# Attention, mixture of experts and dense layer in one kernel: a smaller second run and two decoded units moved ahead of a branch

## The chip, the cores and the metric

One core of a Trainium2 chip runs the whole program in one launch. The metric is the device time of that launch in microseconds (us). The kernel before took 637.18 us, the median of three executions (636.78 to 637.54).

The engines are named as the profile names them: PE is TensorE (matrix products), DVE is VectorE, ACT is ScalarE, POOL is GpSimd, SP is SyncE, which here issues most of the DMAs.

## The reference

```python
attn = softmax(rot(q) @ rot(k).T / 8) @ v          # 2 x 8 heads, 576 rows, 64 columns
x    = attn as 1152 rows x 512                     # all heads of a row side by side
nl   = x @ w_gate + log1p(exp(x @ w_noise)) * noise    # 8 experts
top2 = two largest of nl in each row, weights = softmax over the two
for each expert e, for its rows:  out += weight * (relu(x @ w1[e]) @ w2[e])   # 512 -> 1024 -> 512
h = out @ w_in                                     # 512 -> 2048, w_in and w_out in 64-bit floats
y = (max(h, 0) + log1p(exp(-|h|))) @ w_out         # 2048 -> 512
```

Everything is computed in 32-bit precision: a product of two 32-bit matrices is made of three products of a high and a low part (high by high, high by low, low by high).

## The kernel before

The kernel has three stages in time. Up to about 168 us it computes the attention, in an order that is written out by hand: the string `ORDER` names each piece of work, and the engines take their pieces in that order (each engine works strictly in its own order). `plan` gives for every piece its engine and what has to stand ahead of it.

From 168 to about 423 us it works through nine runs of expert rows. Run 0 takes one expert's rows of the first 512 tokens, and is part of `ORDER` (`G0` to `G7`), so that it starts before the routing of all tokens is known. Runs 1 to 8 take the eight experts in order of their number of rows. Run 1 takes what is left of run 0's expert, with the same weights. `CAPS` gives the rows each run has room for, 192 for run 0 and 256 for run 1 in the kernel before; `RTILES` the 128-row tiles they make (two for both). An expert with more rows than that is completed by `overflow()`, under a branch (line 1447) that tests `mxi`, the largest excess. All five engines load `mxi` (line 1446) and take the branch each for itself. When it isn't taken, each engine adds to its own semaphores what the skipped instructions would have added, after its own earlier instructions have ended.

A run is 14 to 17 slots. The first eight are `gemm1` (line 1264 on): for each 128 of the 1024 hidden columns, 12 products (4 pieces of 512 by 3 parts) over all rows of the run. Then comes `gemm2`: for each tile of rows 24 products 512 columns wide, three parts with a slot after each. A tile of at most 64 rows has another form (lines 1290 to 1297): high and low part of its rows lie side by side in one stationary operand, and two products of a kind take the place of three, 16 in all. `xg_T` transposes the gathered rows of the next run in between.

In the slots the other engines prepare what comes: `split_hi` and `split_lo` (lines 189 and 193) split a 512 KB chunk of weights into high and low part, on ACT and DVE. The 64-bit matrices are decoded in 32 units: `dec_load` (a DMA on SP's queue, lines 215 and 218), `dec_a` (two ACT instructions, lines 227 and 228), `dec_b` (two DVE instructions, lines 235 and 236, and one on POOL, line 239), `dec_c` (a DMA to `wtab`, line 244). `dec_at` says in which slot each step stands; the first two units were loaded just ahead of run 1 and decoded in it.

From 423 us to the end the dense layer runs on `wtab`.

The memory of the attention's pools is given to later pools. `pa` holds the two output tiles of run 0 (`y0`, `y1`) and is closed before `mo`, which holds among others the row buffers `xg` of the gathers, the outputs `y`, and the eight buffers `hb` of `gemm1`'s results.

Of the kernel before, what the change touches and what calls it, by code (L numbers as in the profile page):

```python
# [11 lines left out]
F32 = mybir.dt.float32  # L12
# [3 lines left out]
I32 = mybir.dt.int32  # L16
U32 = mybir.dt.uint32
AF = mybir.ActivationFunctionType
OP = mybir.AluOpType
# [4 lines left out]
B, H, S, D = 2, 8, 576, 64  # L24
N, DM, E, F1 = B * S, H * D, 8, 1024
# [3 lines left out]

CAPS = (192, 256, 256, 288, 288, 320, 320, 320, 384)
NR = len(CAPS)
RTILES = [-(-c // 128) for c in CAPS]
ROW0 = [sum(RTILES[:r]) for r in range(NR)]
# [52 lines left out]
T14,5 Th14,4 X12 Th14,5 Tl14,4 X13 E70 Tl14,5 E71 T15,0 Xd12 T15,1 rs15 Th15,0 Xd13 l12 A14,1 Th15,1 Tl15,0 l13 ld3  # L88
sl1 Tl15,1 T15,4 Ao14,1 A14,0 Th15,4 XT0 Tl15,4 Ao14,0 z1 T15,2 XTh0 sl2 Th15,2 T15,3 XTl0 A15,0 Th15,3 Tl15,2 Tl15,3
XT1 Ao15,0 XTh1 A15,1 sp3 XTl1 ri14 ld5 X14 sl3 Ao15,1 sp4 X15 Xd14 ri15 l14 ld6 G0 Xl15 l15 Xd15 m0 sl4 G1 Gh0 sp5  # L90
Gl0 m1 ld7 G2 Gh1 m2 Gl1 G3 Gh2 xo13 Gl2 m3 sl5 mP4 Gh3 xo15 sp6 Gl3 G4 mF4 m6 G5 Gh4 Gl4 m7 G6 Gh5 oa1 oa0 G7 Gh6 sp7
Gl5 mP8 mF8 Gl6 Gh7 ga1 sl6 k0 sl7 Gl7 k1 k2 k3
"""


def in_order(plan):
    names = [re.match("([A-Za-z]+)(.*)", x).groups() for x in ORDER.split()]
    keys = [(kind, *map(int, rest.split(","))) for kind, rest in names]
    assert len(set(keys)) == len(keys) == len(plan)
    place = {k: i for i, k in enumerate(keys)}  # L100
    assert all(place[d] < place[k] for k in keys for d in plan[k][2])
    return keys
# [3 lines left out]
def fused_kernel(ctx: ExitStack, tc: tile.TileContext, q, k, v, w_gate, w_noise, noise, w1, w2,  # L106
                 w_in, w_out, cs_t, out):
    nc = tc.nc
# [3 lines left out]
    def ap(t, off, dims):  # L112
        return bass.AP(tensor=t.tensor, offset=t.offset + off, ap=dims)
# [3 lines left out]
    wtab = dram.tile([16 * 128, 1024], F32, name="wtab")  # L117
# [28 lines left out]
    pools = {}  # L146
# [55 lines left out]
    def split_chunk():  # L202
        split_hi()
        split_lo()

    dec = {}
    w_in64, w_out64 = w_in.bitcast(I32), w_out.bitcast(I32)

    def dec_load(u):
        c, half = divmod(u, 2)  # L210
        j, isout = divmod(c, 2)
        x = pools["dc"].tile([128, 512, 2], I32, name="x64")
        if isout:
            src = ap(w_out64, (j * 256 + half * 128) * DM * 2, [[2 * DM, 128], [1, 2 * DM]])
            nc.sync.dma_start(out=x.rearrange("p a b -> p (a b)"), in_=src)
        else:
            src = ap(w_in64, (half * 256 * F2 + j * 256) * 2, [[2 * F2, 128], [2 * 128 * F2, 2], [1, 512]])
            nc.sync.dma_start(out=x.rearrange("p (k a) b -> p k (a b)", k=2), in_=src)
        dec[u] = [x]

    def dec_a(u):


        (x,) = dec[u]
        a = pools["dc"].tile([128, 512], F32, name="da")
        m = pools["dc"].tile([128, 512], I32, name="dm", bufs=3)
        nc.scalar.activation(a, x[:, :, 1].bitcast(F32), AF.Copy, scale=2.0 ** -112)
        nc.scalar.activation(m, x[:, :, 0].bitcast(U32), AF.Copy, scale=2.0 ** -29)
        dec[u] += [a, m]

    def dec_b(u):
        x, a, m = dec[u]
        t = pools["dc"].tile([128, 512], I32, name="dt", bufs=1)
        ai = a.bitcast(I32)
        nc.vector.tensor_scalar(t, ai, 3, None, op0=OP.logical_shift_left)
        nc.vector.scalar_tensor_tensor(out=ai, in0=ai, scalar=-(1 << 31), in1=t, op0=OP.bitwise_and,  # L236
                                       op1=OP.bitwise_or)

        nc.gpsimd.tensor_tensor(out=m, in0=m, in1=ai, op=OP.add)  # L239

    def dec_c(u):
        c, half = divmod(u, 2)
        m = dec.pop(u)[2]
        nc.sync.dma_start(out=ap(wtab, c * 128 * 1024 + half * 512, [[1024, 128], [1, 512]]), in_=m.bitcast(F32))

    def w1_blk(e, kk, f):
        c = f // 2
# [72 lines left out]
    at1 = at_ctx.enter_context(tc.tile_pool(name="at1", bufs=1))  # L320
# [643 lines left out]
    V, A = nc.vector, nc.scalar  # L964
# [129 lines left out]
    def op(key, eng, cost, after, fn, *args):  # L1094
        plan[key] = (eng, cost, after, lambda: fn(*args))
# [4 lines left out]
    for n in range(NSTEP):  # L1100
        p, h, i = block(n)
# [13 lines left out]
    for g in range(2 * NP_):  # L1115
        p, h = divmod(g, 2)
        for u in range(6 - h):
            n = 5 * g + (0, 1, 2, 3, 3, 4)[u]
# [7 lines left out]
        for a in range(2):  # L1126
            n = 5 * g + 3 + a
# [335 lines left out]
    def gather(r):  # L1463
        for t in range(RTILES[r]):
            m = min(CAPS[r] - 128 * t, 128)
            XG[r, t] = mo.tile([128, DM], F32, name="xg", bufs=4)
            gather_rows(XG[r, t][:m], idxr[:m, r - 2, t:t + 1])

    near1 = mo.tile([128, 1], I32, name="near1", bufs=1)
    off1, x1 = (mo.tile([128, 1], F32, name=n, bufs=1) for n in ("off1", "x1"))  # L1470
    to1, toT = (mo.tile([128, 128], F32, name=n, bufs=1) for n in ("to1", "toT"))
# [9 lines left out]

    NDEC = 32
    slot0 = [sum(8 + 3 * RTILES[q] for q in range(1, r)) for r in range(NR)]
    dec_slot = [slot0[r] + o for r in range(1, NR) for o in ((9, 12) if r == 1 else (2, 4, 9, 12, 16)) if o < 8 + 3 * RTILES[r]][:NDEC]
    dec_at = {}
    for u, s0 in enumerate(dec_slot):
        dec_at.setdefault(s0, []).append((dec_a, u))
        dec_at.setdefault(s0 + 1, []).append((dec_b, u))
        dec_at.setdefault(s0 + 2, []).append((dec_load, u + 2))
        dec_at.setdefault((dec_slot[u + 1] if u + 1 < NDEC else s0 + 1) + 2, []).append((dec_c, u))  # L1490

    def slot(limit):
        n = slot_no[0]
# [53 lines left out]
        nc.scalar.activation(dh, ps, AF.Copy)  # L1547
        nc.vector.tensor_tensor(out=dl, in0=ps, in1=dh.bitcast(F32), op=OP.subtract)

    dec_load(0)  # L1550
    dec_load(1)
    when = ((0, 1), (0, 2), (1, 1))
    ends = {(0, 2): [lambda: scale0(0), lambda: ygather(0, 1), lambda: ygather(1, 1)], (1, 0): [lambda: scale0(1)],
            (1, 2): [lambda: let_loads(YG[1, 1])], (2, 0): [lambda: combine(0), lambda: combine(1)],
# [177 lines left out]
```

## Time and profile before

| what | value |
|---|---|
| times of three executions | 637.18, 637.54, 636.78 us |
| the profiled execution | 636.7 us, of which the span from the first to the last instruction is 634.9 us |
| PE busy | 615.6 us, 97% of the span |
| DVE, ACT, POOL busy | 481.5 us (76%), 424.2 us (67%), 215.8 us (34%) |
| HBM read and written | 76.5 MB and 23.6 MB |

Busy time of PE is the time in which at least one product is under way. Products overlap, so the cost of one in a row of many is the distance from its start to the next start, which is shorter than its duration.

### The profile page before, as it was taken

To read this page: it belongs to the slowest core of one execution; us is meant where nothing else is said; L and a number is where in the kernel's file an instruction comes from. 1 tells how busy PE (TensorE), PEld (TensorE's weight loads), DVE (VectorE), ACT (ScalarE), POOL (GpSimd) and SP (SyncE) were. 2 spreads that over 40 slices of the span, in tenths; PEclk is the share of its full clock that TensorE was granted. 3 is DMA by queue.
4 is the path that set the end of the run, shared out by engine and by line. 5 is a ranking of instruction groups with operands and counts; after the bars stand their busy time and mean duration, and the time that the engine had idled before them with its cause. 6 is when DMAs were issued, how large, how long until landed. Compare 5 with 4: busy or idle time off the path is not lost.

```text
span 634.9 us, 11660 instructions
## 1 busy us (share of the span) xinstructions
PE 615.6 (97%) x3992; PEld 558.3 (88%) x3992; DVE 481.5 (76%) x984; ACT 424.2 (67%) x893; POOL 215.8 (34%) x306
## 2 busy tenths in 40 slices
PE   3899999999999999999999999999999999999997
PEld 3799999999989989797989888988889998899996
DVE  6889999998776887777868676739987656776664
ACT  3999899899635677576757575648766545655553
POOL 6976785864561324333241413214200000000000
PEclk9999999999999999999999999999999999999999
DMA  4556555787429799979999997667301100100000
GB/s 134 148 124 141 137 153 134 221 233 245 139 75 350 238 348 318 330 270 364 302 339 305 326 297 262 222 237 201 103 1 51 34 1 1 51 1 2 34 2 33
DMA packets 70066, 109.59 MB, mean 173 GB/s; under 512 B 11733, under 2 KB 39253, under 8 KB 69621
## 3 DMA queue, kind: packets, MB, share of 16 engines
q1 hardware_dynamic: 63428, 92.85, 47.2%
q0 software_dynamic: 3136, 10.10, 4.9%
q10 hardware_dynamic: 3440, 5.88, 2.5%
q8 instruction: 32, 0.52, 0.4%
q14 instruction: 30, 0.24, 0.1%
HBM read 76.50 MB, written 23.59 MB: 158 GB/s over the span
## 4 chain that ended last, share of the span: by engine, by line
PE 60%; ACT 4%; DVE 4%; DMA 1%; issue 1%; SPq 0%; ACTq 0%; DVEq 0%
PE p L270 10%; PE p L271 10%; PE p L272 10%; PE po L271 4%; PE po L272 4%; PE po L270 4%; PE ph L270 4%; PE ph L271 4%; PE ph L272 4%; PE p L1295 2%; PE p L1297 1%; PE pa L1259 1%; DMA x<-in_moe_w_in_dram 1%; DVE wc L193 1%; ACT wb L189 1%
## 5 line engine op out<-in xcount | busy, mean ns | idle before, releaser
L239 POOL TENSOR_TENSOR dm<-dm,da 128x512 int32<-128x512 int32 x32 | 42.0, 1311 | 127.9 <-DVE da L236 57.6
L1607 ACT ACTIVATE fa<-ph 128x256 f32<-128x256 f32 (+1 forms) x64 | 26.0, 407 | 63.5 <-PE ph L272 63.5
L502 DVE TENSOR_REDUCE nmx<-ps 128x1 f32<-128x576 f32 x72 | 53.8, 751 | 4.4 <-PE ps L489 4.0
L511 ACT ACTIVATE P<-ps,nmx 128x576 f32<-128x576 f32 x72 | 53.6, 746 | 4.9 <-DVE nmx L502 4.3
L1277 DVE SCALAR_TENSOR_TENSOR hb<-p,hb 128x256 fp32r<-128x256 f32 (+1 forms) x104 | 31.7, 347 | 30.4 <-ACT hb L1275 30.4
L193 DVE TENSOR_TENSOR w<-wraw,w 128x1024 fp32r<-128x1024 f32 x39 | 51.8, 1335 | 1.6 <-PE p L272 0.9
L1614 DVE TENSOR_SCALAR fu<-fa 128x256 f32<-128x256 f32 (+1 forms) x64 | 19.9, 311 | 42.3 <-ACT fa L1608 42.2
L556 DVE TENSOR_TENSOR ptl<-pt,pth 128x512 fp32r<-128x512 f32 x72 | 48.2, 685 | 4.9 <-ACT pth L552 4.1
L189 ACT ACTIVATE w<-wraw 128x1024 fp32r<-128x1024 f32 x42 | 44.5, 1062 | 9.6 <-DMA wraw<-in_moe_w_dram 7.3
L271 PE MATMUL p<-xl,w 128*128 128x256 f32 (+3 forms) x152 | 46.3, 304 | 0.3 <-DVE xl L1262 0.3
L552 ACT ACTIVATE pth<-pt 128x512 fp32r<-128x512 f32 x72 | 42.9, 602 | 5.1 <-PE pt L520 4.7
L270 PE MATMUL p<-xh,w 128*128 128x256 f32 (+3 forms) x152 | 46.3, 305 | 0.0
L272 PE MATMUL p<-xh,w 128*128 128x256 f32 (+3 forms) x152 | 46.2, 304 | 0.0
L193 DVE TENSOR_TENSOR wb<-wraw,wb 128x1024 fp32r<-128x1024 f32 x33 | 45.0, 1371 | 0.7 <-ACT wb L189 0.7
L1518 POOL DMA_INDIRECT yg<-ytab,yrow x17 | 17.5, 1031 | 80.2 <-DVE fu L1614 35.6
L520 PE MATMUL pt<-ident,P 128*128 128x128 f32 x288 | 42.9, 274 | 1.1 <-DVE ptl L556 0.4
L189 ACT ACTIVATE wb<-wraw 128x1024 fp32r<-128x1024 f32 x33 | 34.9, 1060 | 3.9 <-DMA wraw<-in_moe_w_dram 3.3
L1615 DVE TENSOR_TENSOR fa<-fa,fu 128x256 f32<-128x256 f32 (+1 forms) x64 | 29.4, 460 | 9.8 <-ACT fl L1609 8.0
L520 PEld LDWEIGHTS pt<-ident,P 128*128 128x128 f32 x288 | 33.5, 141 | 3.3 <-DVE ptl L556 1.1
L1275 ACT ACTIVATE hb<-p 128x320 fp32r<-128x320 f32 (+3 forms) x64 | 26.0, 424 | 14.1 <-PE p L272 13.4
L1626 ACT ACTIVATE gh<-fl 128x256 fp32r<-128x256 f32 (+1 forms) x64 | 27.7, 433 | 10.5 <-DVE fl L1620 10.5
L489 PE MATMUL ps<-wb,yg 128*128 128x288 f32 (+1 forms) x160 | 30.4, 319 | 2.8 <-ACT P L511 1.4
(385 smaller groups left out, 2176.9 us busy)
## 6 DMA issues: line engine op xcount, KB each, us to landing
wraw<-in_moe_w_dram SPq DMA_DIRECT2D x64, 512.0 KB, 4.7
x<-in_moe_w_in_dram SPq DMA_DIRECT2D x16, 512.0 KB, 6.3
x<-in_moe_w_out_dram SPq DMA_DIRECT2D x16, 512.0 KB, 5.8
wtab<-dm SPq DMA_DIRECT2D x32, 256.0 KB, 5.3
wraw<-wtab SPq DMA_DIRECT2D x16, 512.0 KB, 4.5
ytab<-y ACTq DMA_DIRECT2D x18, 256.0 KB, 4.6
ytab<-wb SPq DMA_DIRECT2D x4, 1024.0 KB
wb<-wb SPq DMA_DIRECT2D x6, 640.0 KB
```

What stands on the lines that cost most here:

```text
L189: nc.scalar.activation(hi, r, AF.Copy)
L193: lo_eng.tensor_tensor(out=lo, in0=r, in1=hi.bitcast(F32), op=OP.subtract)
L239: nc.gpsimd.tensor_tensor(out=m, in0=m, in1=ai, op=OP.add)
L270: nc.tensor.matmul(ps, ah, bh, start=first and i == 0, stop=False)
L271: nc.tensor.matmul(ps, ah, bl, start=False, stop=False)
L272: nc.tensor.matmul(ps, al, bh, start=False, stop=last and i == n - 1)
L502: nc.vector.tensor_reduce(out=nmx, in_=stS[n][:, :, :HN], axis=AX.XY, op=OP.max, negate=True)
L511: nc.scalar.activation(P_of(n).rearrange("p (a c) -> p a c", a=2), ps[:, :, :HN], AF.Exp, bias=nmx, scale=1.0, accum_out=acc)
L520: nc.tensor.transpose(ps[:, kb, :], Pt[:, kb * 128:(kb + 1) * 128], ident)
L552: nc.scalar.activation(dh, x, AF.Copy)
L556: nc.vector.tensor_tensor(out=dl, in0=x, in1=dh.bitcast(F32), op=OP.subtract)
L1277: nc.vector.scalar_tensor_tensor(out=o, in0=ps[:, c], scalar=0.0, in1=hh[:, c].bitcast(F32), op0=OP.max, op1=OP.subtract)
```

## The change

Run 1 gets room for 192 rows in place of 256. Two units of the 64-bit matrices (`NEAR = 2`) become pieces of `ORDER`: their loads `dl` on SP after the last store of attention rows, `da` on ACT, `db` on DVE, and `dp` on POOL, which also issues the store to `wtab` on POOL's queue. They use the memory of the attention's tile `pth` (`spare`). `db` and `dp` stand at the end of `ORDER`, after the routing's last pieces `k2` and `k3`. Run 1 decodes nothing any more, run 2 three units in place of four, run 8 two in place of one; the loads of the third and fourth unit stand in run 1. The tiles `y` of `mo` are allocated first, so that they, and not `xg`, lie where run 0's output tiles lie.

```diff
-CAPS = (192, 256, 256, 288, 288, 320, 320, 320, 384)
+CAPS = (192, 192, 256, 288, 288, 320, 320, 320, 384)
...
-Gl0 m1 ld7 G2 Gh1 m2 Gl1 G3 Gh2 xo13 Gl2 m3 sl5 mP4 Gh3 xo15 sp6 Gl3 G4 mF4 m6 G5 Gh4 Gl4 m7 G6 Gh5 oa1 oa0 G7 Gh6 sp7
-Gl5 mP8 mF8 Gl6 Gh7 ga1 sl6 k0 sl7 Gl7 k1 k2 k3
+Gl0 m1 ld7 G2 Gh1 m2 Gl1 G3 Gh2 xo13 Gl2 m3 sl5 mP4 Gh3 xo15 dl0 dl1 sp6 Gl3 G4 mF4 m6 G5 Gh4 Gl4 m7 G6 Gh5 oa1 oa0 G7
+Gh6 sp7 Gl5 mP8 mF8 Gl6 Gh7 da0 da1 ga1 sl6 k0 sl7 Gl7 k1 k2 k3 db0 dp0 db1 dp1
...
+    def spare(i, n=1):
+        if not room:
+            room.append(at1.tile([128, 2, 4, S], F32, name="pth").rearrange("p a b c -> p (a b c)"))
+        return room[0][:, 512 * i:512 * (i + n)].bitcast(I32)
...
-        x = pools["dc"].tile([128, 512, 2], I32, name="x64")
+        if u < NEAR:
+            x = spare(2 * u, 2).rearrange("p (a b) -> p a b", b=2)
+        else:
+            x = pools["dc"].tile([128, 512, 2], I32, name="x64")
...
-        a = pools["dc"].tile([128, 512], F32, name="da")
-        m = pools["dc"].tile([128, 512], I32, name="dm", bufs=3)
+        if u < NEAR:
+            a, m = spare(4 + 2 * u).bitcast(F32), spare(5 + 2 * u)
+        else:
+            a = pools["dc"].tile([128, 512], F32, name="da")
+            m = pools["dc"].tile([128, 512], I32, name="dm", bufs=3)
...
-    def dec_b(u):
+    def dec_b(u, part=2):
         x, a, m = dec[u]
-        t = pools["dc"].tile([128, 512], I32, name="dt", bufs=1)
+        if part == 1:
+            nc.gpsimd.tensor_tensor(out=m, in0=m, in1=a.bitcast(I32), op=OP.add)
+            dec_c(u, nc.gpsimd)
+            return
+        t = spare(u) if u < NEAR else pools["dc"].tile([128, 512], I32, name="dt", bufs=1)
...
+        if part == 0:
+            return
         nc.gpsimd.tensor_tensor(out=m, in0=m, in1=ai, op=OP.add)
...
-    def dec_c(u):
+    def dec_c(u, eng=nc.sync):
...
+    for u in range(NEAR):
+        op(("dl", u), "SP", 2300, [("A", 14, 0), ("A", 14, 1), ("A", 15, 0), ("A", 15, 1), ("xo", 15)], dec_load, u)
+        op(("da", u), "ACT", 1310, [("dl", x) for x in range(u + 1)], dec_a, u)
+        op(("db", u), "DVE", 1200, [("da", x) for x in range(NEAR)], dec_b, u, 0)
+        op(("dp", u), "POOL", 1330, [("db", u)], dec_b, u, 1)
...
+    mo.tile([128, DM], F32, name="y", bufs=2)
...
-    dec_slot = [slot0[r] + o for r in range(1, NR) for o in ((9, 12) if r == 1 else (2, 4, 9, 12, 16)) if o < 8 + 3 * RTILES[r]][:NDEC]
-    dec_at = {}
-    for u, s0 in enumerate(dec_slot):
+    dec_in = {2: (2, 7, 11), 8: (2, 4)}
+    dec_slot = [slot0[r] + o for r in range(2, NR) for o in dec_in.get(r, (2, 4, 9, 12, 16))]
+    dec_at = {slot0[2] - 6: [(dec_load, NEAR)], slot0[2] - 4: [(dec_load, NEAR + 1)]}
+    for u, s0 in enumerate(dec_slot, NEAR):
...
-    dec_load(0)
-    dec_load(1)
```

## Rows read from the trace of the kernel before

**Rows 1.** The page: busy time, share of the span and instructions of each engine.
```profile
PE 615.6 (97%) x3992; PEld 558.3 (88%) x3992; DVE 481.5 (76%) x984; ACT 424.2 (67%) x893; POOL 215.8 (34%) x306
```

**Rows 2.** Waits of PE: engine, line, releaser: us in total, times, longest.
```profile
PE pa L1259 <- ACTq L1447: 0.6, 1, 0.6
...
PE p L271 <- DVE xl L1262: 0.3, 1, 0.3
```

**Rows 3.** Window after the branch: length, busy us of each engine, clock, DMA share, GB/s.
```profile
190.00:200.00 10.00, 10.00 (x82) 9.68 (x81) 6.70 (x11) 5.98 (x10) 0.72 (x1) 1.00 0.99 344
```

**Rows 4.** Timeline of PE (start, duration): 192 columns (run 0), then 256 (run 1).
```profile
169.78 0.28 PE L270 MATMUL pa<-yg,w 128*128 128x192 f32 x1
...
171.45 0.28 PE L270 MATMUL pa<-yg,w 128*128 128x192 f32 x1
...
191.14 0.28 PE L270 MATMUL p<-xh,w 128*128 128x256 f32 x1
...
202.35 0.40 PE L270 MATMUL p<-w,hb 128*128 128x512 f32 x1
```

**Rows 5.** Timeline of PE: run 1's second tile in `gemm2`, and the transposes' two sizes.
```profile
163.85 0.46 PE L1055 MATMUL pa<-ident,w 64*128 64x64 f32 x4
...
206.53 0.60 PE L1259 MATMUL pa<-ident,xg 128*128 128x128 f32 x4
...
209.03 0.39 PE L271 MATMUL p<-w,hb 128*128 128x512 f32 x1
...
214.39 0.28 PE L270 MATMUL p<-xh,wb 128*128 128x256 f32 x1
```

**Rows 6.** Timeline of PE at the branch, and of DVE's last instruction before it.
```profile
187.93 1.06 PE L1259 MATMUL pa<-ident,yg 128*128 128x128 f32 x8 [0.56 <-ACTq L1447]
...
186.06 0.33 DVE L682 TENSOR_REDUCE idxr<-tq 128x21 int32<-128x168 f32 x1
```

**Rows 7.** Lines 1447 and 1446: durations (ns), first and last start.
```profile
L1447 SPq EVENT_SEMAPHORE  x6: 17/17/17, 191.7 to 192.7; - x6
...
L1447 DVEq EVENT_SEMAPHORE  x2: 21/21/21, 187.3 to 187.4; - x2
...
L1446 DVEq TENSOR_LOAD <-mxi x1: 544/544/544, 186.1 to 186.1; - x1
```

**Rows 8.** Timelines of DVE and POOL: a decoded unit alone, then two back to back.
```profile
211.63 0.42 DVE L235 TENSOR_SCALAR dt<-da 128x512 int32<-128x512 int32 x1
212.09 0.69 DVE L236 SCALAR_TENSOR_TENSOR da<-da,dt 128x512 int32<-128x512 int32 x1
212.69 0.15 DVE L911 TENSOR_SCALAR off<-yrow 128x1 f32<-128x1 int32 x1
...
212.93 1.29 POOL L239 TENSOR_TENSOR dm<-dm,da 128x512 int32<-128x512 int32 x1 [11.15 <-DVE x L912]
...
238.65 0.42 DVE L235 TENSOR_SCALAR dt<-da 128x512 int32<-128x512 int32 x1
239.17 1.59 DVE L236 SCALAR_TENSOR_TENSOR da<-da,dt 128x512 int32<-128x512 int32 x1
...
238.67 1.54 POOL L239 TENSOR_TENSOR dm<-dm,da 128x512 int32<-128x512 int32 x1 [9.31 <-DVE da L236]
```

**Rows 9.** Timeline of ACT around `da`'s place, and the page's DMA issues.
```profile
186.02 0.60 ACT L1304 ACTIVATE y<-p 128x512 f32<-128x512 f32 x1 [4.80 <-PE p L272]
...
x<-in_moe_w_in_dram SPq DMA_DIRECT2D x16, 512.0 KB, 6.3
```

**Rows 10.** Timeline of PE where run 3 begins.
```profile
238.19 0.29 PE L270 MATMUL p<-xh,w 128*128 128x288 f32 x1
238.79 0.40 PE L271 MATMUL p<-xl,w 128*128 128x288 f32 x1 [0.30 <-DVE xl L1262]
```

**Rows 11.** POOL's first gather after the branch; a store's issue on SP.
```profile
199.28 1.11 POOL L1036 DMA_INDIRECT xg<-xtab,idxr  x1 [12.82 <-DMA ytab<-y]
...
214.25 0.34 SPq L244 DMA_DIRECT2D wtab<-dm  x1
```

More of the change, by code (lines that the diff above doesn't have):

```diff
@@ L204, in split_chunk @@
         split_lo()
+    NEAR = 2
     dec = {}
     w_in64, w_out64 = w_in.bitcast(I32), w_out.bitcast(I32)
+    room = []
+    def spare(i, n=1):
+        if not room:
+            room.append(at1.tile([128, 2, 4, S], F32, name="pth").rearrange("p a b c -> p (a b c)"))
+        return room[0][:, 512 * i:512 * (i + n)].bitcast(I32)
     def dec_load(u):
@@ L237, in dec_b @@
                                        op1=OP.bitwise_or)
+        if part == 0:
+            return
         nc.gpsimd.tensor_tensor(out=m, in0=m, in1=ai, op=OP.add)
-    def dec_c(u):
+    def dec_c(u, eng=nc.sync):
         c, half = divmod(u, 2)
         m = dec.pop(u)[2]
-        nc.sync.dma_start(out=ap(wtab, c * 128 * 1024 + half * 512, [[1024, 128], [1, 512]]), in_=m.bitcast(F32))
+        eng.dma_start(out=ap(wtab, c * 128 * 1024 + half * 512, [[1024, 128], [1, 512]]), in_=m.bitcast(F32))
     def w1_blk(e, kk, f):
@@ L1483, in fused_kernel @@
     slot0 = [sum(8 + 3 * RTILES[q] for q in range(1, r)) for r in range(NR)]
-    dec_slot = [slot0[r] + o for r in range(1, NR) for o in ((9, 12) if r == 1 else (2, 4, 9, 12, 16)) if o < 8 + 3 * RTILES[r]][:NDEC]
-    dec_at = {}
-    for u, s0 in enumerate(dec_slot):
+    dec_in = {2: (2, 7, 11), 8: (2, 4)}
+    dec_slot = [slot0[r] + o for r in range(2, NR) for o in dec_in.get(r, (2, 4, 9, 12, 16))]
+    assert len(dec_slot) == NDEC - NEAR
+    dec_at = {slot0[2] - 6: [(dec_load, NEAR)], slot0[2] - 4: [(dec_load, NEAR + 1)]}
+    for u, s0 in enumerate(dec_slot, NEAR):
         dec_at.setdefault(s0, []).append((dec_a, u))
@@ L1489, in fused_kernel @@
         dec_at.setdefault(s0 + 2, []).append((dec_load, u + 2))
-        dec_at.setdefault((dec_slot[u + 1] if u + 1 < NDEC else s0 + 1) + 2, []).append((dec_c, u))
+        dec_at.setdefault((dec_slot[u + 1 - NEAR] if u + 1 < NDEC else s0 + 1) + 2, []).append((dec_c, u))
     def slot(limit):
```

## Prediction, made before the changed kernel was run

> **What bounds the kernel now.** I read the page first: PE is busy for 615.6 of 634.9 us, no other engine above 481.5 [rows 1]. A busy share alone proves little, so the waits of PE come next: from 187 us to the dense layer two are left, 0.6 us at the branch and 0.3 us where run 3 begins [rows 2]. In the stretch that the change touches PE is busy for 10.00 of 10 us at a granted clock of 1.00, while DVE and ACT have 6.70 and 5.98; the DMA share is 0.99, but PE waits for no weights there [rows 3]. So between the branch and the dense layer a product saved on PE is time saved, and a stall of PE is time lost, one for one. All below is worked out on the profiled execution: 636.7 us, with a span of 634.9, so 1.8 us lie around the span and stay. It stands 0.5 us under the median of 637.18; I carry the difference over to the median.
>
> **What run 1 saves on PE.** `gemm1` keeps its 96 products, each 192 columns wide in place of 256. With 192 columns, 15 steps from 169.78 to 171.45 give 0.111 us a product; with 256, 96 steps from 191.14 to 202.35 give 0.117 [rows 4]. A quarter of the columns saves only 5%: 96 x 0.0055 = 0.5 us. `gemm2`'s second tile has 64 rows left and takes the narrow form, 16 products in place of 24. They are 512 columns wide as before, at (214.39 - 209.03) / 23 = 0.233 us each [rows 5], so 8 x 0.233 = 1.9 us. The four transposes of that tile are 0.60 us with 128 rows and 0.46 with 64 [rows 5]: 0.1 us. Sum: 2.5 us, and I see no way for it to be much else, since all three forms stand in the trace. Chunks for run 2 are no hindrance: PE reaches them 2.5 us sooner, but waits for none now [rows 2], and run 1 is freed of two units' ACT and DVE work.
>
> **The 0.3 us at run 3's start.** PE waits there for `xl` of the third tile [rows 10]; on DVE `xl` comes just ahead of a unit's `dt` at 238.65 [rows 8], in a row of work that is late because run 2 has four units. With three, the last decoded after that tile's `xl`, I take the wait to go: 0.3 us (0 to 0.6, the distance 238.19 to 238.79). PE's own order is next there, at no cost.
>
> **The branch.** This is what the change adds. In the compiled program of the kernel before, the first transpose after the branch waits for DVE's count from inside the skipped part (`overflow` reads a PSUM tile of the same pool with DVE). DVE supplies it when it passes the branch, and only after its own earlier instructions have ended. Before, DVE's last instruction starts at 186.06 and ends at 186.39 [rows 6], the load of `mxi` runs beside it from 186.1 and takes 0.544 us, and DVE supplies its count at 187.3 [rows 7]. PE then has only its own 0.56 us of crossing and starts at 187.93; the releaser that the profile names, ACT, passes only about then [rows 6].
>
> The change puts `db0` and `db1` between `k2` and the load of `mxi` on DVE, and `dp0` on POOL beside them. A unit alone is: `dt` 0.46 us to the start of `da`, 0.60 from there to the next instruction, and POOL's addition 1.30 us after `dt`'s start [rows 8]. Of two units back to back the rows show more: POOL's addition for the first begins at 238.67 under the second `dt`, and the second `da`, issued at 239.17, takes 1.59 us in place of 0.69 and ends 0.55 us after the addition (238.67 + 1.54 = 240.21). DVE's `da` stands still while POOL adds [rows 8]. So with `dt0` at 186.3: `da0` 186.8, `dt1` 187.4, `dp0` asks at 187.6, and `da1` ends 240.76 - 238.65 = 2.1 us after `dt1`'s start, at 189.5. DVE passes the branch then, and not at 187.3. PE before had about 0.19 us from that check to its first transpose (the crossing's rest; an estimate from 187.93 against the last PE event of the branch at 187.6 and two checks behind it), so it starts at 189.7 or 189.8 in place of 187.93: **1.85 us lost**. If `da1` were not held, DVE's crossing would follow the load of `mxi`, issued with `da1` at 187.9 in place of 186.06, so 1.85 us later at 189.1, and PE would lose 1.45. If the load were hidden as well, `da1` ends at 188.6 and PE loses 0.95. The upper end is that PE waits for POOL too: rival C. I take 1.85, since the row with two units is this very sequence. Behind the waiting transposes PE holds the rest of run 0 (10 products) and all of run 1; ACT's `xh` and DVE's `xl` wait for them, as before.
>
> **The other edits, at nothing.** ACT sits idle for 4.80 us ahead of 186.02 [rows 9], and `da0` and `da1` take some 2.7 there (estimate from their two ACT instructions' 0.67 each). Their loads are issued near 171 behind the last store of attention rows; with 6.3 us to landing [rows 9] they are in by 178, in a stretch with a low DMA share, so DVE is not held. Without this cover `db` would start late, and each us would be a us. `dp1` and the stores run on POOL after the branch has long been reached; POOL's first gather now waits 12.82 us for run 0's outputs [rows 11], and with `y` laid there it comes at about 193 in place of 199.28. PE needs these rows near 206, so that gain is hidden too. The 1.5 MB of the two units leave a stretch at 0.99 DMA share [rows 3], which nobody on PE waits for. The unit added in run 8 finds ACT and DVE idle for nearly half of the time.
>
> **Sum.** -0.5 - 1.9 - 0.1 - 0.3 + 1.85 = -0.95 us: 635.7 by the profiled execution, **636.2** by the median. Its own range is 635.6 to 636.9 (stall 1.45 to 2.2).
>
> **Rivals.** *B, the branch is free.* If PE's wait on DVE fell away or `db` found its place before 186.3, the 2.8 us stay whole: 634.4. For it: the profile names ACT, not DVE, as what ended the wait [rows 2]. Against it: DVE works without a pause until 186.39 [rows 6], and `db` is last in its order.
>
> *C, PE waits for POOL too: slower.* The place is the same first transpose (or `xl` behind it), the price is POOL's way to the branch: `dp1` can begin at 189.65 and takes 1.3; its two stores are issued on POOL's queue, between 0.34 us (an issue on SP) and 1.11 (POOL's gather) each [rows 11]; load and crossing 1.2 (186.1 to 187.3). That is 192.5 to 194, a stall of 4.8 to 6, and a net loss of 2 to 3.2: 639.2 to 640.4. It decides as soon as anything ahead of `gemm1` counts POOL beyond `k3`. Against it: SP crosses at 191.7 [rows 7], 3.8 us after PE has gone on, and nobody is held, so a crossing binds only him who needs that engine's count. The Trainium skill (SBUF — State Buffer, section "SBUF: two separate sides") says that the descriptors of a DMA issued from GpSimd are written by GpSimd itself, and that a VectorE instruction in a two-port mode locks it out meanwhile; by that the upper price would be nearer, and no run here shows a plain store on POOL. In my forecast it costs nothing.
>
> *D, run 1's buffers are late.* By their sizes the fourth and fifth `hb` lie on the decoded units' `m`, which their stores must have left. Stores issued at 190 to 192.5 land by 199 with the gather's or load's 6.3 us; `gemm1` (from 193.0, 1.34 us a block) writes there at 198.4 and 199.7. Four PSUM buffers hide some 4 us more. If the landing takes over 10 us, up to 1.5 us are lost: 636.2 to 637.7.
>
> *E, 192 rows are not enough.* Then `overflow` runs, with 4 MB of weights in a row; at 344 GB/s [rows 3] alone 12 us: over 648. With the reference's inputs (seed 0) 163 rows are left for run 1, so it should not.
>
> **How the numbers follow.** Chances: forecast 0.60, B 0.17, C 0.11, D 0.10, E 0.02. A difference under 0.2%, 1.3 us, can hardly be told from none; that border is 635.9. Of the forecast's 0.60 some 0.21 lies under it, with B 0.38 faster; C, E and 0.04 of D give 0.17 slower; the rest is 0.45. The range 634.4 to 637.9 holds the forecast, B's value and most of D; it leaves out C and E.
>
> **What would show it.** After: DVE's four decode instructions between 186.3 and 189.5, the second `da` near 1.6 us; the first transpose of line 1259 at 189.7; `gemm1` of run 1 at 0.111 us a product, 10.7 in all; run 2's first product 0.65 us before 214.39; no wait for `xl` at run 3. Wrong: a first transpose before 188.5 (B) or after 191 (C), or a wait of PE within run 1 (D).

## The result, and the profile after

The changed kernel took 640.56 us (median of six runs, 639.45 to 641.03), the kernel before 636.97 (six runs on the same chip, 636.28 to 637.54). The ratio is 1.0055, with a 95% interval of 1.0042 to 1.0068: 3.6 us slower. The forecast was 636.2, in a range of 634.4 to 637.9, so it was wrong, in sign and in size. The profiled execution took 641.03 us, with a span of 639.2 against 634.9.

In the changed kernel's profile every line number is larger: 1259 (transposes) has become 1285, `gemm1`'s 270 to 272 are 290 to 292, `hb` (1275, 1277) is 1301 and 1303, `gemm2`'s narrow form (1295, 1297) is 1321 and 1323, and the branch (1447) is 1473. The units decoded ahead of the branch appear as tile `pth`.

PE's busy time is the same as in [rows 1], in a longer span:

```profile
PE 616.2 (96%) x3984; PEld 558.9 (87%) x3984; DVE 479.6 (75%) x993; ACT 423.0 (66%) x893; POOL 215.1 (34%) x308
```

The waits of PE from the branch to the end (engine, tile, line, releaser: us in total, times, longest) were 0.6 and 0.3 in [rows 2]:

```profile
PE pa L1285 <- DVEq L1473: 2.4, 1, 2.4
PE ph L290 <- ACT w L189: 1.4, 1, 1.4
PE p L290 <- ACT hb L1301: 0.9, 1, 0.9
PE p L290 <- DVE hb L1303: 0.7, 1, 0.7
```

The first is the branch, the second the dense layer's start, the other two lie in run 1. The wait at run 3 is gone. The branch itself, as a timeline (start, duration), answers to [rows 6] and [rows 8]:

```profile
187.32 0.42 DVE L253 TENSOR_SCALAR pth<-pth 128x512 int32<-128x512 int32 x1
187.57 1.28 POOL L248 TENSOR_TENSOR pth<-pth 128x512 int32<-128x512 int32 x1 [1.18 <-DVE pth L254]
187.77 1.63 DVE L254 SCALAR_TENSOR_TENSOR pth<-pth 128x512 int32<-128x512 int32 x1
189.16 0.65 POOL L264 DMA_DIRECT2D wtab<-pth  x1 [0.30 <-POOL pth L248]
189.72 1.02 PE L1285 MATMUL pa<-ident,yg 128*128 128x128 f32 x8 [2.41 <-DVEq L1473]
...
191.41 0.59 POOL L264 DMA_DIRECT2D wtab<-pth  x1 [0.30 <-POOL pth L248]
```

Behind it, the chain of work that ended last in 185 to 215 us (start, duration, what) shows what run 1 then waited for:

```profile
191.41 6.68 DMA wtab<-pth
...
198.33 0.07 ACT hb L1301
...
203.01 6.78 DMA wraw<-in_moe_w_dram
209.79 0.02 issue
209.81 1.06 ACT w L189
210.87 0.23 ACT hb L1301
```

The second unit's store leaves POOL at 191.41 and lands 6.68 us later; only then ACT writes the first `hb` of run 1, at 198.33 in place of 193.34. (The timeline of ACT puts this wait down to another DMA, `ytab<-y`. The chain names the store, and so does ACT's own row in e3_run8, where that `hb` starts at 198.10.) ACT takes its work in order, so the splits of run 2's chunks stand behind that `hb`, the next loads go out late, and one that is issued at 203.01 holds ACT again until 209.81. PE stands still both times, first within `gemm1`, which takes 11.67 us (10.70 in e1_caps below), then within `gemm2`:

```profile
193.08 0.25 PE L290 MATMUL p<-xh,w 128*128 128x192 f32 x1
...
204.75 0.41 PE L290 MATMUL p<-w,hb 128*128 128x512 f32 x1
...
211.14 0.50 PE L290 MATMUL p<-wb,hb 128*128 128x512 f32 x1 [0.88 <-ACT hb L1301]
...
216.06 0.28 PE L290 MATMUL p<-xh,wb 128*128 128x256 f32 x1
```

Where the time went is read from PE's first product of each stage, here for both kernels and, in advance, for the experiments (us of each profile; the last column is the way from run 8's `gemm2` to the first dense `gemm2`):

```
                run 1   run 2   run 3   run 3 gemm2   dense gemm1   dense gemm2   end of run 8 to there
before          191.14  214.39  238.19  251.67        424.09        430.31        25.16
changed         193.08  216.06  240.18  253.09        427.06        434.75        28.20
e1_caps         191.25  212.13  235.99  251.68        424.10        430.72        25.56
e3_run8         193.17  215.37  239.60  252.51        424.91        431.11        25.14
e5_hb_order     194.69  215.57  239.40  252.31        426.44        432.55        26.78
e7_one_add      193.87  215.88  239.98  252.89        426.80        432.94        26.59
e8_before_run8  190.96  214.21  238.02  250.93        425.11        432.76        28.38
e9_three        192.62  213.51  238.18  251.09        423.50        429.70        25.15
e10_less_dve    190.87  212.43  236.71  250.89        423.67        429.90        25.17
e6_loads_ahead  191.15  213.53  238.26  251.17        423.57        430.08        25.45
e11_ahead_y     190.89  211.78  236.90  249.81        422.21        428.44        25.17
```

The changed kernel lost 1.94 us at the branch, won 0.27 in run 1 (2.5 were forecast), lost 0.32 in run 2, won 0.57 in run 3's `gemm1` (12.91 us for 13.48), and lost 3.04 at the dense layer's start (the last column). That is 4.5 us, against 4.3 between the spans.

The last loss has two parts. Windows of the changed kernel there (length, busy us of PE, PEld, DVE, ACT, POOL, granted clock, DMA share, GB/s):

```profile
424.00:427.00 3.00, 1.66 (x9) 1.05 (x7) 1.91 (x3) 3.00 (x5) 0.00 (x0) 1.00 0.94 381
427.00:432.00 5.00, 4.79 (x25) 4.62 (x26) 3.95 (x7) 2.74 (x5) 0.00 (x0) 0.66 0.94 281
```

PE first idles for 1.4 us, and then the granted clock is down: by the trace's record of the granted clock it was at 0.5 (the lower level, 1.2 GHz in place of 2.4) for 3.41 us from 428.1. By the timeline of ACT, what PE waits for is a chunk's split:

```profile
409.54 1.06 ACT L189 ACTIVATE w<-wraw 128x1024 fp32r<-128x1024 f32 x1 [0.39 <-DMA wraw<-wtab]
...
424.00 1.06 ACT L189 ACTIVATE w<-wraw 128x1024 fp32r<-128x1024 f32 x1 [5.50 <-DMA wraw<-wtab]
...
425.92 1.06 ACT L189 ACTIVATE w<-wraw 128x1024 fp32r<-128x1024 f32 x1
```

Between 401 and 411 us the changed kernel does four such splits into `w`, the kernel before five: one chunk fewer is ready when the loads are held at run 8's end, and two splits into `w` instead of one are left for after 423 us. PE waits for the second.

### The profile page after: what moved, and what is told of

Same layout as the page of the kernel before. It is cut to its first block, busy times and chain, and to the rows that moved or that the text cites. A ratio compares the mean times of both kernels' runs of the same rounds, so it can differ in the third digit from the quotient of the medians.

```text
span 639.2 us, 11656 instructions
## 1 busy us (share of the span) xinstructions
PE 616.2 (96%) x3984; PEld 558.9 (87%) x3984; DVE 479.6 (75%) x993; ACT 423.0 (66%) x893; POOL 215.1 (34%) x308
## 4 chain that ended last, share of the span: by engine, by line
PE 58%; ACT 5%; DMA 4%; DVE 3%; issue 1%; POOL 0%; SPq 0%; ACTq 0%; DVEq 0%
PE p L290 9%; PE p L291 9%; PE p L292 9%; PE ph L291 4%; PE ph L290 4%; PE ph L292 4%; PE po L291 4%; PE po L292 4%; PE po L290 4%; PE p L1321 2%; PE p L1323 2%; PE pa L1285 1%; DMA wraw<-in_moe_w_dram 1%; DMA wtab<-pth 1%; ACT wc L189 1%; ACT wb L189 1%
## 5 line engine op out<-in xcount | busy, mean ns | idle before, releaser
L259 POOL TENSOR_TENSOR dm<-dm,da 128x512 int32<-128x512 int32 x30 | 39.1, 1304 | 133.4 <-DVE da L254 51.9
L1303 DVE SCALAR_TENSOR_TENSOR hb<-p,hb 128x256 fp32r<-128x256 f32 (+2 forms) x112 | 31.7, 326 | 34.6 <-ACT hb L1301 34.6
L290 PE MATMUL p<-xh,w 128*128 128x288 f32 (+4 forms) x152 | 46.2, 304 | 0.7 <-DVE hb L1303 0.7
L292 PE MATMUL p<-xh,w 128*128 128x288 f32 (+4 forms) x152 | 46.0, 303 | 0.0
L291 PE MATMUL p<-xl,w 128*128 128x288 f32 (+4 forms) x152 | 46.0, 302 | 0.0
L1301 ACT ACTIVATE hb<-p 128x320 fp32r<-128x320 f32 (+4 forms) x64 | 25.7, 412 | 17.0 <-PE p L292 12.1
```

The source lines that it names most:

```text
L290: nc.tensor.matmul(ps, ah, bh, start=first and i == 0, stop=False)
L291: nc.tensor.matmul(ps, ah, bl, start=False, stop=False)
L292: nc.tensor.matmul(ps, al, bh, start=False, stop=last and i == n - 1)
L1303: nc.vector.scalar_tensor_tensor(out=o, in0=ps[:, c], scalar=0.0, in1=hh[:, c].bitcast(F32), op0=OP.max, op1=OP.subtract)
```

## The experiments

Each was timed in rounds, in turn with the kernel before. Theory A was formed from the traces above: run 1's saving is real; the branch, the `hb` buffers and run 8's missing split take it away. The table has medians, in us, and ratios to the kernel before on the same chip with their 95% intervals. The experiments ran on several chips, so their times are compared by the ratios:

```
e1_caps         638.85  1.0035  1.0024 to 1.0045     e9_three        636.60  0.9995  0.9986 to 1.0005
e2_caps_y       638.64  1.0036  1.0023 to 1.0049     e10_less_dve    636.54  0.9999  0.9990 to 1.0009
e3_run8         638.67  1.0027  1.0017 to 1.0037     e11_ahead_y     635.55  0.9982  0.9973 to 0.9991
e5_hb_order     639.41  1.0043  1.0028 to 1.0058     e12_ahead_early 643.08  1.0103  1.0088 to 1.0119
e6_loads_ahead  635.67  0.9985  0.9976 to 0.9994     e13_both        635.75  0.9986  0.9977 to 0.9995
e7_one_add      641.62  1.0077  1.0063 to 1.0091     e14_dec_behind  635.56  0.9982  0.9973 to 0.9991
e8_before_run8  638.63  1.0021  1.0012 to 1.0030     e15_dec_first   637.13  1.0005  0.9994 to 1.0016
```

### e1_caps and e2_caps_y: the smaller run 1 alone

```diff
-CAPS = (192, 256, 256, ...
+CAPS = (192, 192, 256, ...
```

e2_caps_y has this line too, ahead of `near1`:

```diff
+    mo.tile([128, DM], F32, name="y", bufs=2)
```

> The kernel before with one edit: run 1 holds 192 rows. No unit ahead of the branch, row buffers and decoding as before. Theory A (run 1's saving is real; in the changed kernel it is eaten by the branch, by an hb buffer that waits for the units' second store, and by one split too few ahead of the dense layer): no stall of PE in run 1, run 2 starts 2.4 to 2.6 us sooner than before's 214.39, and the end comes 2.5 to 2.8 us sooner: about 634.3 against 637.0. Rival B (PE is now faster than run 2's weights, which arrive at a DMA share near 1, so that run 1 stalls whatever the decoding does): PE waits for hb or w in run 1 here too, and the gain is under 1 us: 636.0 to 637.0.

> As e1_caps, with y laid first, so that xg and hb lie 4 KB higher as in the changed kernel; still no unit ahead of the branch. Theory A: the address alone costs nothing without the units' stores; first hb of run 1 within 1.5 us of where e1_caps has it, time within 0.5 us of e1_caps, about 634.3. Rival D (the new place of hb itself is the fault, because it lies on the skipped part's weight tile and so waits for SP's crossing of the branch): first hb only after 195, PE stalls 0.5 us or more in run 1, 635 to 636.

Both theories missed the end. Run 1 had no stall, as A said and B did not, and run 2 began 2.26 us sooner (A: 2.4 to 2.6). But run 3's `gemm2` began at 251.68, where before had 251.67, and the kernel was slower than before, not faster. In e1_caps the whole saving stops at run 3's start, by the waits of PE and by its timeline:

```profile
PE p L271 <- DVE xl L1262: 2.5, 1, 2.5
```

```profile
235.99 0.30 PE L270 MATMUL p<-xh,w 128*128 128x288 f32 x1
...
238.80 0.40 PE L271 MATMUL p<-xl,w 128*128 128x288 f32 x1 [2.51 <-DVE xl L1262]
```

In [rows 10] the same product starts at 238.79 after a wait of 0.30. PE came 2.2 us sooner and `xl` did not come sooner at all. DVE's timeline says why: between the two last `xl` of run 3 it has a split and a unit to do, at the very times of the kernel before (its split starts at 236.18 there):

```profile
235.58 0.69 DVE L1262 TENSOR_TENSOR xl<-pa,xh 128x512 fp32r<-128x512 f32 x1 [2.45 <-ACT xh L1261]
236.19 1.22 DVE L193 TENSOR_TENSOR w<-wraw,w 128x1024 fp32r<-128x1024 f32 x1
237.32 0.42 DVE L235 TENSOR_SCALAR dt<-da 128x512 int32<-128x512 int32 x1
237.85 0.69 DVE L236 SCALAR_TENSOR_TENSOR da<-da,dt 128x512 int32<-128x512 int32 x1
238.46 0.28 DVE L1262 TENSOR_TENSOR xl<-pa,xh 128x128 fp32r<-128x128 f32 x1
```

and the windows of e1_caps show DVE nearly full from 210 to 230, and then the DMA engines:

```profile
210.00:220.00 10.00, 10.00 (x78) 9.34 (x77) 9.60 (x29) 7.84 (x16) 3.73 (x3) 1.00 0.67 223
220.00:230.00 10.00, 10.00 (x64) 8.85 (x63) 9.79 (x15) 5.16 (x9) 5.48 (x5) 1.00 0.88 287
230.00:240.00 10.00, 7.49 (x39) 5.80 (x38) 7.20 (x11) 6.42 (x11) 1.33 (x1) 1.00 1.04 369
```

In the kernel before DVE was busy for 9.23 and 9.41 us in the first two. PE's 10.00 of 10 was therefore no proof that PE alone was the bound: the row of loads, splits and units behind it had no slack either, and the 0.3 us at run 3 was where the two met. Part of DVE's load there is POOL's: in run 2 of e1_caps two splits that run while POOL adds take 1.95 and 1.94 us, in place of 1.21 for one alone. The narrow tile also costs DVE 1.3 us more in run 1 (16 pieces of `hb` with 3.99 us in place of 8 with 3.37, and a subtraction for `y` of 0.68 at 214.52).

e2_caps_y has the same time and no stall in run 1 (its one new wait, 0.7 us, lies in run 2): the addresses alone cost nothing, so rival D of these two expectations is refuted for it. In the changed kernel SP is across the branch at 195.7, 2.6 us before the first `hb`, so SP is not what that `hb` waits for there either (in e15_dec_first, below, it is). Up to the dense layer e1_caps is level with before; its 2.0 us by the median are not explained by its trace, which is of an execution of 637.52. Its eleven runs spread over 637.14 to 640.92 where before's twenty-one lie within 636.38 and 637.27. Each run has a mean granted clock on record: 0.998 or 0.999 in five of the eleven (637.14 to 639.07), 0.994 to 0.997 in the other six (638.73 to 640.92), never under 0.998 in before's. So a lowered clock goes with part of the 2.0 us; where it fell in those runs no trace shows.

### e3_run8 and e8_before_run8: the unit in run 8

```diff
-    dec_in = {2: (2, 7, 11), 8: (2, 4)}
+    dec_in = {2: (2, 5, 8, 11), 8: (2,)}
```

That is e3_run8, in the changed kernel. e8_before_run8 does the reverse in the kernel before: its `dec_slot` gives run 2 the slots (2, 7, 11) in place of (2, 4, 9, 12), and so run 8 the slots (2, 4).

> The changed kernel with one unit moved back from run 8 to run 2 (run 2: four units, run 8: one). Theory A: one more split is done in run 8 before loads are held, PE no longer idles 1.4 us at the dense layer's start and the granted clock stays 1.00 there, so 2.5 to 3 us come back: 637.6 to 638.1; the run-1 stalls stay. Rival C (the dense layer's first chunks land late because the loads are held and started later, not because a split is missing): the wait of ACT for the load and PE's idle time at the dense layer stay, 640.0 to 641.0.

> The kernel before with one edit: run 2 decodes three units in place of four, and run 8 two in place of one. Theory A (the slot in run 8 that decodes does no split, so one chunk fewer is split when loads are held, and the dense layer waits for a late chunk): PE idles 1.2 to 1.6 us at the dense layer's start and loses 2.5 to 3 us there; run 3's stall of 0.3 us may go, which gives back 0.3: 638.5 to 640.0. Rival C (that loss was of the changed kernel's other edits): time within 0.6 us of before, 636.2 to 637.4.

Theory A's account of the dense layer held in both, rival C's in neither. e3_run8 has no wait of PE at the dense layer, a granted clock of 1.00 there, and 25.14 us in the table's last column, as before. e8_before_run8 has the loss without any other edit, with 28.38 in that column:

```profile
PE ph L270 <- ACT w L189: 1.6, 1, 1.6
```

and by windows the lowered clock behind it:

```profile
425.00:430.00 5.00, 4.74 (x25) 4.57 (x26) 4.07 (x7) 2.78 (x6) 0.00 (x0) 0.66 0.89 282
```

e3_run8 got back 3.2 us by the profiles and, from 1.0055 to 1.0027, about 1.8 by the ratios, less than the 2.5 forecast. e5_hb_order and e7_one_add below keep the added unit, PE waits 1.6 and 1.3 us there for the same split, and the clock stays at 1.00: their last column is 26.78 and 26.59. So the missing split costs some 1.5 us in these traces, and twice that where the clock fell behind it. e8_before_run8 also shows the other half of that edit: with three units in run 2 the wait at run 3 goes, and `gemm1` there takes 12.91 us in place of 13.48.

### e5_hb_order: the buffers that wait

```diff
-        hb = pool.tile([128, 2 * CAP], F32R, name="hb", bufs=8)
+        hb = pool.tile([128, 2 * CAP], F32R, name=f"hb{7 - f}", bufs=1)
...
+    for b in range(8):
+        mo.tile([128, 2 * CAP], F32R, name=f"hb{b}", bufs=1)
```

> The changed kernel with hb's eight buffers used from the other end: the first two of run 1 now lie behind the decoded units' tile, the third is the first that lies on it. Nothing else changes. Theory A: the first hb starts near 194.5 in place of 198.33, PE's 0.85 us in gemm1 of run 1 go, and so does most of the 1.04 us in gemm2, whose weights were loaded late because ACT stood behind that hb: 638.7 (639.7 if only the first stall goes). Rival B (loads, not the buffer): the hb starts earlier, but PE's idle time in run 1 stays near 1.9 us in sum: 640.2 to 640.8.

Both of PE's waits in run 1 are gone: from run 1's first product to run 2's it takes 20.88 us in place of 22.98, 2.1 us less. That is theory A's case, and not B's. The first `hb` starts at 196.87, before the second store has landed, so its wait for that store is gone. Run 1 begins 1.6 us later here than in the changed kernel, which alone could have hidden part of the wait; e9_three has the same order of buffers, begins run 1 at 192.62 and takes 20.89 us to run 2. The median came down by only 1.15 us, and the ratio's interval overlaps the changed kernel's (1.0042 to 1.0068), so in time this gain isn't clear of the noise. This profile shows something new at the branch, as a window says:

```profile
190.00:194.00 4.00, 4.00 (x16) 2.73 (x15) 1.02 (x2) 0.98 (x2) 1.83 (x2) 0.57 0.89 254
```

After the same idle time of 2.4 us as in the changed kernel the granted clock went to 0.5 for 3.41 us, which there it did not. Among the seven runs the two with a mean granted clock of 1.000 took 637.99 and 638.18 us, the one with the lowest, 0.992, took 641.76.

### e7_one_add: DVE and POOL at the branch

```diff
-            nc.gpsimd.tensor_tensor(out=m, in0=m, in1=a.bitcast(I32), op=OP.add)
-            dec_c(u, nc.gpsimd)
-            return
+            if u == 0:
+                return
+            v = room[0][:, 2048:4096].bitcast(I32).rearrange("p (u k c) -> p u k c", u=2, k=2)
+            nc.gpsimd.tensor_tensor(out=v[:, :, 1], in0=v[:, :, 1], in1=v[:, :, 0], op=OP.add)
+            dec_c(0, nc.gpsimd)
+            dec_c(1, nc.gpsimd)
+            return
```

> The changed kernel with POOL's two additions ahead of the branch joined into one instruction for both units, which therefore starts only when DVE has done the second unit. Same arithmetic. Theory A (the second da on DVE stands still while POOL adds): the second da falls from 1.63 us to 0.69, PE's first transpose after the branch comes 0.9 us sooner than 189.72; the stores leave about 1 us later than 189.16 and 191.41 on the mean, and the first hb of run 1 waits for them as before, so that little of the 0.9 us reaches the end: 639.5 to 640.6. Rival H (da is slow for another reason, or PE waits for POOL after all): da stays above 1.2 us, or the transpose moves with POOL's later end, to 190.5 or more.

The timeline of e7_one_add:

```profile
187.47 0.69 DVE L258 SCALAR_TENSOR_TENSOR pth<-pth 128x512 int32<-128x512 int32 x1
188.33 2.35 POOL L251 TENSOR_TENSOR pth<-pth 128x1024 int32<-128x1024 int32 x1 [2.24 <-DVE pth L258]
188.97 1.04 PE L1289 MATMUL pa<-ident,yg 128*128 128x128 f32 x8 [1.98 <-DVEq L1477]
```

Without POOL beside it the second `da` takes 0.69 us in place of 1.63: A's collision is shown, and rival H refuted, since PE goes on 1.7 us before POOL's addition ends. The Trainium skill (SBUF — State Buffer, section "SBUF: two separate sides") calls the port pair that VectorE and GpSimd share a lock, held for a whole instruction. The durations agree with that: in the changed kernel POOL's addition starts first, at 187.57, and `da` ends 0.55 us after it. PE's transposes came 0.75 us sooner, 0.29 of it because DVE's row started sooner in this execution; behind `da` now stands the crossing itself. The time got worse all the same, by more than expected. The profiled execution, 639.96 us, is the fastest of the five, and 1.1 us under the changed kernel's own, so its trace does not show what the median lost. In it the clock fell to 0.5 for 3.41 us after the branch, and the stores left later, the first by 1.8 us and the second by 0.2; neither was tested alone, and the cause stays open.

### e9_three: all three costs taken away

It joins the edits of e3_run8, e5_hb_order and e7_one_add in the changed kernel.

> The changed kernel with three edits together: hb's buffers from the other end (e5_hb_order), one unit back from run 8 to run 2 (e3_run8), POOL's two additions joined (e7_one_add). It still holds 192 rows in run 1 and still decodes two units ahead of the branch. Theory A with F (all that is left against before is about 1 us at the branch, run 1's saving counts because the two units' loads are out of the stream): run 3 starts at 237.0 to 238.0, no stall of PE above 0.5 us between the branch and the dense layer, end 635.6 to 636.4. If the costs don't add up (a stall returns at run 3 or the clock is lowered after the branch): 637.5 to 639.

From 1.0055 the ratio comes down to 0.9995: the three together take away the whole of the loss against the kernel before. They don't add up, since alone they changed the ratio by -0.0028, -0.0012 and +0.0022, and no run leaves one of the three out, so how much each gives in the company of the others isn't known. Run 3 begins at 238.18 and the time is 636.60, both 0.2 outside what was expected, with 2.0 us of PE still idle at the branch, here without a fall of the clock, and 0.6 for an `xl` at run 2's start.

### e6, e10, e11, e13, e14, e15, e12: what holds run 3

e6_loads_ahead is e1_caps with the loads of the first two units ahead of the branch; they are decoded at run 1's slots 3 and 5, the loads of the next two stay at slots 11 and 14:

```diff
+        if u < 2:
+            x = mx.tile([128, 4, CAP], F32R, name=("xh", "xl")[u]).rearrange("p a b -> p (a b)")[:, 0:1024]
...
     slot_no = [0]
+    dec_load(0)
+    dec_load(1)
```

e10_less_dve is e1_caps, and e13_both is e11_ahead_y, with an edit that leaves out DVE's two decoding instructions for run 2's four units, so that these units' values are not decoded:

```diff
+        if u not in (2, 3, 4, 5):
             nc.vector.tensor_scalar(t, ai, 3, None, op0=OP.logical_shift_left)
...
```

e11_ahead_y is e6_loads_ahead with `y` first, as in e2_caps_y. e14_dec_behind is e11_ahead_y with

```diff
-        dec_at.setdefault(s0 + 1, []).append((dec_b, u))
+        dec_at.setdefault(s0 + (3 if s0 == slot0[2] + 9 else 1), []).append((dec_b, u))
```

e15_dec_first is e11_ahead_y with run 1's units at slots (0, 2), and e12_ahead_early is it with units at (1, 3, 9, 12) in run 1, the later two loaded at slots 4 and 6, and (5, 11) in run 2.

> The kernel of e1_caps with one thing moved: the 1 MB that decoded units 0 and 1 load goes out on SP ahead of the branch (near 171 us, into the second xh and xl buffers, which nobody holds until run 2's rows), in place of just behind it; the units are decoded in run 1 as before, near its start. No decoding ahead of the branch, no early store. e1_caps showed run 1's 2.2 us of saving stop at run 3, where PE waits 2.5 us for xl. Theory F (the stretch from the branch to run 3 is bound by the stream of loads, at a DMA share near 1, and only 1 MB less in it lets run 3 start sooner): chunk loads are issued 2 us or more sooner near 232 than e1_caps's 231.37 and 233.25, PE's wait for xl falls under 0.6 us, run 3's gemm2 starts 2 us sooner than 251.68, and the end is 634.3 to 635.0. Rival G (xl of run 3 is late by the order on ACT and DVE, where run 2's four units stand ahead of it): the wait for xl stays above 1.5 us and the time at 637 to 639.

> The kernel of e1_caps without DVE's two decoding instructions for run 2's four units (dt and da, 1.1 us a unit, 4.5 us in all); their loads, ACT's and POOL's part and their stores stay, so the table's values for these units are not decoded. In e1_caps DVE is busy for 9.6 of 10 us from 210 to 220 and 9.8 from 220 to 230, and chunk loads go out when DVE has split the one before. Theory J (run 3 starts when DVE's queue allows it, and that is where run 1's saving stops): PE's wait of 2.5 us for xl falls to 0.5 or less, run 3's gemm2 starts 1.5 to 2.2 us sooner than e1_caps's 251.68, end 634.6 to 636. Rival F (it is the bytes of the loads): all stays, wait 2 us or more, 251 or later, 638 to 639.

> e6_loads_ahead with y laid first, so that run 2's gather needn't wait until run 0's output rows are stored. In e6_loads_ahead PE waits 0.9 us for that gather in run 1, and 0.6 us for xl at run 3. Theory J: the 0.9 us go, but the end moves little, as run 3 starts when DVE's queue allows it: within 0.5 us of e6_loads_ahead, 635.2 to 636.2. Rival (PE's own order is the bound again): the 0.9 us come back in full, 634.6 to 634.9.

> e11_ahead_y with DVE's work spread to where it waits: run 1 decodes four units (slots 1, 3, 9, 12; the loads of the later two at slots 4 and 6) and run 2 two, in place of two and four. Theory J: less of DVE's queue stands ahead of run 3's xl; PE's wait there goes below 0.3 us and run 3 starts up to 2 us sooner than e6_loads_ahead's 238.26: 634.0 to 635.2. Rival F (loads bind, and two unit loads now go into run 1, at a DMA share near 1): chunk loads later, waits of PE in run 1 or 2, 636 to 638.

> e11_ahead_y with e10_less_dve's edit: DVE's decoding instructions for run 2's four units are left out (these units' table values are not decoded). Against e1_caps's 251.68, run 3's gemm2 began 0.8 us sooner with DVE relieved (e10) and 1.9 us sooner with the loads ahead and y first (e11). If the loads and DVE's queue each bind in their turn (theory K), the two together give more than either, 2.3 us or more: wait for xl under 0.4 us, gemm2 of run 3 at 249.3 or sooner, end 634.4 to 635.2. If one of them alone is the bound and e11 has already freed it, nothing is added: gemm2 at 249.6 to 250.0, wait 0.8 to 1.0 us, end 635.3 to 635.8.

> e11_ahead_y with one order changed on DVE and POOL: run 2's third unit is decoded two slots later (slot 12 in place of 10), so that its dt and da stand behind run 3's third xl on DVE and not ahead of it. In e11_ahead_y these two take from 235.25 to 236.39, and PE's wait of 1.0 us for that xl ends with it at 236.67. Theory K: xl comes right behind ACT's xh, at 235.8, and PE's wait falls to 0.4 us or less, end 634.6 to 635.3. If xl is late by what ACT does ahead of it (its xh waits for PE's transposes at 235.05), the wait stays 0.8 us or more and the time at 635.4 to 636.0.

> e11_ahead_y with the two early-loaded units decoded at run 1's slots 0 and 2 in place of 3 and 5. In e11_ahead_y PE's one wait of 1.0 us stands where run 2 begins (211.78 to 213.09, for xl, not at run 3 as I had put it for e13 and e14), DVE is busy for 9.23 of 10 us from 200 to 210, ahead of that xl, and 5.67 from 190 to 200. Theory J (DVE's queue is what PE meets): with 1.1 us of DVE's work, or both units' 2.2, moved from behind 202 to ahead of 200, the wait falls to 0.4 us or less and run 3's gemm2 comes 0.6 to 1.0 us sooner than 249.81: 634.5 to 635.0. Rival F (the loads of the chunks bind): DVE waits for the same landings, the wait stays 0.8 us or more, 635.3 to 636.

e6_loads_ahead lies between its two theories. One of the two loads went out at 173.05, the other only at 186.44. F had the chunk loads go out 2 us sooner, and they did not: counted from the first, the one of 231.37 in e1_caps is the one of 231.97 here, and only the one of 237.54 is sooner, at 236.93. PE reaches run 3 at 238.26, 2.3 us later than in e1_caps, finds `xl` there, and `gemm2` comes 0.5 us sooner. So the 0.5 us are no proof of F. e6_loads_ahead is faster than both kernels.

e10_less_dve took 4.5 us of work from DVE, and of the 2.5 us at run 3 1.0 stayed: `gemm2` came 0.8 us sooner, J's 1.5 to 2.2 and F's none are both missed. The edit relieved DVE by less than it seems. POOL's additions for two of these units now run back to back (from 224.18, 2.56 us for both), and a split of DVE that starts at 223.97 beside them takes 3.85 us in place of 1.21, so that DVE is busy for 10.00 of 10 us from 220 to 230. ACT waits for loads (1.34 and 1.03 us ahead of two splits at 228 and 230).

e11_ahead_y removed the wait for the gather, and run 3's `gemm2` came at 249.81, 1.9 us sooner than before's. Its ratio and e14's are the lowest found, some 1.1 us under the kernel before, but those of e6 and e13 lie within their intervals. The waits of PE from the branch on are

```profile
PE p L275 <- DVE xl L1268: 1.0, 1, 1.0
PE pa L1265 <- ACTq L1453: 0.6, 1, 0.6
PE ph L274 <- DVE fl L1624: 0.3, 2, 0.2
PE po L276 <- DVE gl L1633: 0.2, 1, 0.2
```

and the 1.0 us stands at run 2's start (211.78 to 213.09), not at run 3, as I had taken it when I wrote what to expect of e13 and e14. So these two were aimed at a wait that was gone; neither made a difference to e11, and neither says what holds run 2. e15 was to tell that, and does not: the wait at run 2's start stays, at 1.1 us, but ACT's first `hb` now waits until 194.97 for SP to cross the branch, and PE has a new wait of 1.0 us in run 1. e12 failed by its own making: the fourth unit's `dm` waited 5.9 us for an early unit's store, which I had left at slot 14.

So it is shown that in e1_caps run 1's saving stops at run 3, and that taking work from DVE and loading two units early each bring run 3's `gemm2` forward. By which way the early loads do it, how much belongs to the one and how much to the other, and what makes the wait that is left at run 2 stays open.

## Why the prediction was wrong

**Held.** The branch: PE's first transpose came at 189.72 (forecast 189.7 or 189.8), 1.79 us later than before (1.85), with the second `da` at 1.63 us (1.59 in the row) and `dt`, `da`, `dt`, `da` from 186.24 to 189.40. The sum by rows of two units back to back in [rows 8] was right, and rivals B and C did not occur: the two stores took POOL 0.65 and 0.59 us to issue, it ended the second at 192.0, and PE had gone on. The narrow tile: from its first product to run 2's it takes 3.78 us (212.28 to 216.06) in place of 5.67, 1.89 less (1.9). The wait at run 3 went, in the changed kernel and, with three units alone, in e8_before_run8; it was worth 0.57 us in both rather than 0.3. In the changed kernel three units were not needed for it: PE came 2.0 us later there, and in e3_run8, which comes 1.4 us later than before with four, the wait is gone too. POOL's gather came at 194.35 (forecast 193), and no wait of PE came of it. E did not occur.

**Two steps failed in the changed kernel, and both had been put at nothing in the sum.**

The first is rival D: the right place, with a wrong size and point. I let only the fourth and fifth `hb` wait, for their own units' `m`, with four buffers of PSUM as cover. The wait came at the first `hb`, and for the later of the two stores, whose landing took 6.68 us (I had 6.3). By the sizes the first `hb` lies on the units' tile `pth` but not on that unit's `m`, so the tile seems to count as one; that is read from the order of events here and in e3_run8 and e7_one_add, and was not tested by itself. The wait also held what stands behind `hb` on ACT: splits and with them loads. Price: 2.1 us of PE (e5_hb_order), where I had put up to 1.5 and a chance of 0.10. So run 1 won 0.27 us and not 2.5.

The second is **"the unit added in run 8 finds ACT and DVE idle"**, which was the wrong question. A slot that ends a unit's decoding does no split, so the unit costs a split and not engine time; the chunk is missing where the loads are held. Priced at nothing, it cost 3.0 us at the dense layer's start, 1.4 as idle time of PE and the rest with a lowered clock (e3_run8, e8_before_run8). The code that decides it stood in `slot`.

**A third step is wrong, but cost little here:** the sentence that between the branch and the dense layer a product saved on PE is time saved, one for one, and with it that I saw no way for the 2.5 us to be much else. e1_caps saved 2.26 us up to run 2 and none of it reached run 3's `gemm2`. The rows were there: DVE's row that is late in run 2 [rows 8], the wait at run 3 for it [rows 10], the DMA share of 0.99 [rows 3]. I took the 0.3 us for a small stall to be won, and it was the end of a row of work without slack. A rival for this was missing. In the changed kernel PE starts run 1 some 2 us later, and the sentence would have come closer. From run 1's first product to run 3's `gemm2` it is 60.53 us in the kernel before. It is 57.62 in e5_hb_order, where run 1 starts 3.55 us later than before and all of the saving arrives, and 58.47 in e9_three, where it starts 1.48 later.

The first two together, -0.27 in run 1 for -2.5 and 3.04 at the dense layer for 0, make 5.3 us; the forecast (-0.95) and the difference of the profiles (+4.3) lie 5.25 apart. The rest nearly cancels: the branch took 0.09 us more than forecast, run 2 lost 0.32, and run 3 won 0.27 more.

## What to carry to other kernels

Before a saving on a full engine is counted, move that engine's work forward in thought and ask which row of work must then be ahead of it too: a wait of 0.3 us at the one place where two rows meet can be the whole slack. Where a change adds a piece to a schedule by slots, read what that slot no longer does. And where a tile is put on borrowed room, ask what comes to lie on any part of it later: here the first such buffer waited for the last store out of the whole, and so did all that stood behind it on its engine.

## What the runs showed that I had not expected

The granted clock fell to 0.5 for 3.41 us after idle times of PE of 1.4 us (changed kernel, 428.1), 1.6 us (e8_before_run8, 426.3), 2.0 us (e7_one_add, 189.8) and 2.4 us (e5_hb_order, 190.0), and did not fall after 1.6 us (e5_hb_order at the dense layer), 2.0 us (e9_three at the branch), 2.41 us (changed kernel at the branch) or 2.51 us (e1_caps at run 3). At half speed 3.41 us cost some 1.7 us (an estimate: half of them; run 1 of e5_hb_order began 1.6 us later than the changed kernel's), more than the stall that came before it in two of these cases. So equal stalls cost unequal times, and a trace of one execution does not tell what the median pays.
